# Hashed attention and channel mix on one core: the first head's bucket bits made as rows, and engines and order set anew

## The chip, the cores and the metric

The kernel runs on one core of one Trainium2 chip. The metric is the device time of one execution in microseconds (us), lower is better. The kernel before takes 245.84 us, the median of three runs (245.41 to 245.97). Engines in the text: TensorE (PE; PEld is its weight load), VectorE (DVE), ScalarE (ACT), GpSimd (POOL), SyncE (SP, which only issues DMAs).

## The reference

Two parts run one after the other. First an attention in which a query sees only the keys of its own hash bucket. A bucket is the six signs of the row times a random 64 x 6 matrix. Then a channel mix on the rows of the attention, with the row before.

```python
q, k, v: (4, 8, 768, 64) float32;  proj: (64, 6)
q_bits = (q @ proj) > 0;  k_bits = (k @ proj) > 0          # six bits a row
mask = bucket(q)[:, None] == bucket(k)[None, :]
scores = where(mask, q @ k.T / 8, -1e9)
attn = softmax(scores) @ v                                  # per batch and head
x = attn with the heads side by side                        # (4, 768, 512)
xk, xr = mixes of x and of x shifted by one row, by mu_k and mu_r
r = sigmoid(xr @ w_r)                                       # 512 x 512
out = r * (relu(xk @ w_k) ** 2 @ w_v)                       # 512 x 1024 x 512
```

## The kernel before

**Pairs of heads.** The 32 heads are taken as 16 pairs, n = 0 to 15, four pairs to a batch. q and k of a pair are loaded as rows, 128 partitions by six chunks of 64 columns a head (tiles nat), v likewise (vn). For the scores both have to stand transposed: tile a holds, for each head, 128 partitions by 768 rows of the sequence. Partitions 0 to 63 are the 64 columns scaled by 4 in float16, and partitions 64 to 69 are the six bits as plus or minus a constant. So one product gives the score and, through the bits, a large term that is greatest where the buckets agree. ScalarE's exponential takes the constant off again, and what lies in another bucket comes out as zero.

**Two ways to prepare a pair.** From pair 2 on (`add_prep`) VectorE writes the scaled half (hi, L391) and the rest in float16 (lo, L394) side by side into nh, a DMA transposes nh into a (tr, L398), TensorE multiplies a by the projection (bits, L418), VectorE takes the signs (bx, L421), and GpSimd copies the six rows of each of the four blocks into a (row, L438). hi9, lo9 and so on are those of pair 9. Pairs 0 and 1 (`add_prep_turn`) do without DMA, because the start waits for them. Each block (one side, one head; pair 1 takes both heads in one) goes through: the scaled copy hi into nh (L462); the first turn on TensorE, float32 transposes of nat, three a head (L473, names y); a copy of the result from PSUM, e32 (L477); the bits as rows of the sequence, three small float32 products of 12 columns a head (L481, names x); their signs into nh (ex, L489); the second turn, six float16 transposes of nh (L504, names t); and the copy into a (evt, L509 on VectorE, L511 on ScalarE).

**Scores, softmax, output.** A pair's scores are nine steps of 1024 columns (names sc, L536); each step goes through an exponential on ScalarE (exp, L540). The products with v are six groups of twelve matmuls a pair (oo, L563). v is copied for the first four pairs by GpSimd (va, L343), and summed over the sequence by three additions on GpSimd (vsum, vsumb, vsumc; L349, L352, L355), since its mean is taken off in the later pairs (va on VectorE, L373). rc and ob (L574 to L581) divide by the sum. xt, xs, xz, df, xka, xk, xra, xr (L594 to L636) make the two mixes; xk7 is the last mix that the first products of batch 1 need.

**Channel mix.** Per batch: 16 groups on xk (kp, L651) with a relu on ScalarE (L655) and a square on VectorE (sq, L658); six groups on xr (L671) with a tanh on ScalarE (L674); six groups of eight matmuls on the squares (L684), multiplied on VectorE (os, L691) and stored. The weights arrive as float32 in ten pieces and are cast on GpSimd (wc, L299).

**What sets the order.** Every operation is added to a plan with its engine, and the list ORDER, 1330 numbers written out, is the order in which all are issued; each engine runs its own part of it strictly in that order. BANKS says which bank of PSUM each product uses. Loads, DMA transposes and stores are issued by SP in the same order. ScalarE issues only the first load of k and that of proj. Engines are fixed by the line that adds an operation, by the table TURN (for pairs 0 and 1) and by W_CAST.

In the start, 20 matmuls on zeros (L247, warm-ups) run while the first loads come.

Of the kernel before, what the change touches and what calls it, by code (L numbers as in the profile page):

```python
# [128 lines left out]
def kernel(  # L129
# [13 lines left out]
    nc = tc.nc  # L143
# [188 lines left out]
    def add_v(n):  # L332
# [9 lines left out]
        def f0():  # L342
            nc.gpsimd.tensor_copy(va_t[sa][:, :, :, 0:D], vn)  # L343
# [421 lines left out]
```

## Time and profile before

| | |
|---|---|
| median of three runs | 245.84 us |
| profiled execution, its time | 244.73 us |
| profiled execution, its span | 243.0 us |
| PE busy | 234.2 us, 96% |
| DVE busy | 187.6 us, 77% |
| ACT busy | 182.6 us, 75% |
| POOL busy | 95.9 us, 39% |
| exponentials | 144 of 1.04 us, 139.1 us |
| first exponential starts | 12.78 us |
| granted clock of TensorE | 1.00 throughout |

The span is the part of the profiled execution that the trace covers; its time has some 1.7 us around it. The profiled execution was faster than the median. A matmul's duration in the trace includes its way through the array, so neighbours overlap: four matmuls of 512 columns last 379 ns each but stand 0.86 us apart in the chain. TensorE's share of busy time is therefore no measure of what is left to gain; the stretches with idle time, and who ended it, are.

### The profile page before, as it was taken

Reading aid. Unit: us, or ns where it says so; the run is one execution under the profiler, and the core shown is the slowest. Engines: PE = TensorE matmul, PEld = TensorE weight load, DVE = VectorE, ACT = ScalarE, POOL = GpSimd, SP = SyncE. Lnnn points to the kernel's source line nnn. Section 1 sums busy time; section 2 is a strip of 40 time slices with the busy share of each in tenths; the row PEclk is TensorE's granted clock in tenths of the full one; section 3 lists DMA queues with packets and bytes.
Section 4 is the critical chain, followed back from the end, with each engine's and each line's share of the span. In section 5 each row is a group of like instructions: output and inputs, shape, how many; then the busy total and the mean of one; then the engine's idle time right before and its main releaser. Section 6 shows DMA issues by size and latency. Waiting matters only on the chain.

```text
span 243.0 us, 6250 instructions
## 1 busy us (share of the span) xinstructions
PE 234.2 (96%) x2522; PEld 147.3 (61%) x2522; DVE 187.6 (77%) x388; ACT 182.6 (75%) x242; POOL 95.9 (39%) x150
## 2 busy tenths in 40 slices
PE   8998999999999899999999999999999999999994
PEld 6975676765567446465556665465566765455443
DVE  3489899999899989699999989936745476966142
ACT  3689999999989689698877998777679871165230
POOL 5465797885919673428036230093500000000000
PEclk9999999999999999999999999999999999999999
DMA  6989999999999999999989683464310403041033
GB/s 229 370 243 197 219 259 230 356 204 348 245 217 233 367 281 208 259 272 264 222 195 233 155 162 85 146 114 126 120 46 0 35 3 119 0 173 47 0 131 132
DMA packets 72526, 44.01 MB, mean 181 GB/s; under 512 B 54832, under 2 KB 67504, under 8 KB 72496
## 3 DMA queue, kind: packets, MB, share of 16 engines
q1 hardware_dynamic: 72272, 43.40, 70.7%
q8 instruction: 20, 0.33, 0.6%
q10 hardware_dynamic: 224, 0.20, 0.2%
q14 instruction: 10, 0.08, 0.1%
HBM read 24.12 MB, written 6.29 MB: 125 GB/s over the span
## 4 chain that ended last, share of the span: by engine, by line
PE 55%; DVE 6%; DMA 3%; issue 1%; DVEq 0%
PE ps_all L684 15%; PE ps_all L651 13%; PE ps_all L536 11%; PE ps_all L671 8%; PE ps_all L563 6%; DMA a<-nh 3%; PE ps_all L418 2%; DVE xk L636 1%; DVE tm L633 1%; DVE nh L391 1%; DVE nh L394 1%; DVE df L622 0%; DVE os L691 0%; DVE va L373 0%; DVE bx L421 0%
## 5 line engine op out<-in xcount | busy, mean ns | idle before, releaser
L540 ACT ACTIVATE pt<-ps_all 128x1024 bf16<-128x1024 f32 x144 | 139.1, 1040 | 19.8 <-PE ps_all L536 18.7
L536 PE MATMUL ps_all<-a 128*128 128x256 f16 (+1 forms) x384 | 79.2, 325 | 2.0 <-ACT pt L540 1.1
L438 POOL COPY a<-bx 6x384 f32<-6x384 f32 x56 | 38.9, 696 | 54.5 <-DVE bx L421 42.3
L563 PEld LDWEIGHTS <-pt 128*128 128x128 bf16 x1152 | 43.7, 97 | 11.6 <-issue 2.1
L651 PE MATMUL ps_all<-xk,wk 128*128 128x384 bf16 x256 | 49.6, 326 | 0.3 <-DVE xk L636 0.3
L536 PEld LDWEIGHTS <-a 128*128 128x128 f16 x384 | 33.7, 98 | 24.9 <-issue 3.5
L684 PE MATMUL ps_all<-wv,k 128*128 128x512 bf16 (+2 forms) x208 | 46.7, 363 | 0.0
L563 PE MATMUL ps_all<-va,pt 128*128 128x65 bf16 x1152 | 46.2, 193 | 0.4 <-DVE va L373 0.4
L658 DVE TENSOR_TENSOR k<-kr 128x384 bf16<-128x384 bf16 x64 | 25.8, 424 | 14.1 <-ACT kr L655 13.8
L655 ACT ACTIVATE kr<-ps_all 128x384 bf16<-128x384 f32 x64 | 29.6, 497 | 7.7 <-PE ps_all L651 6.7
L651 PEld LDWEIGHTS <-wk 128*128 128x128 bf16 x256 | 24.0, 98 | 15.5 <-issue 0.3
L674 ACT ACTIVATE rs<-ps_all 128x512 f32<-128x512 f32 x24 | 14.3, 603 | 23.0 <-DVE os L691 11.7
L684 PEld LDWEIGHTS <-k 128*128 128x128 bf16 x208 | 19.6, 98 | 19.1
L691 DVE SCALAR_TENSOR_TENSOR os<-rs,ps_all 128x512 f32<-128x512 f32 (+2 forms) x26 | 16.7, 643 | 14.9 <-PE ps_all L684 10.8
L394 DVE SCALAR_TENSOR_TENSOR nh<-nat,nh 128x1536 f16<-128x1536 f32 (+1 forms) x16 | 25.7, 1607 | 0.2
L671 PE MATMUL ps_all<-wr,xr 128*128 128x512 bf16 x96 | 24.5, 379 | 0.0
L349 POOL TENSOR_TENSOR vt<-vn 128x384 f32<-128x384 f32 x12 | 14.4, 1200 | 10.8 <-DMA vn<-in_v_dram 7.1
L581 DVE TENSOR_TENSOR ob<-ps_all,rc 128x384 bf16<-128x384 f32 x32 | 17.5, 552 | 0.7
L391 DVE TENSOR_SCALAR nh<-nat 128x1536 f16<-128x1536 f32 (+1 forms) x16 | 15.8, 989 | 1.5 <-DMA nat<-in_k_dram 0.9
L671 PEld LDWEIGHTS <-xr 128*128 128x128 bf16 x96 | 8.7, 97 | 9.5 <-issue 0.6
L421 DVE TENSOR_SCALAR bx<-ps_all 128x768 uint16<-128x768 uint16 x14 | 13.3, 952 | 1.2 <-PE ps_all L418 0.8
L373 DVE SCALAR_TENSOR_TENSOR va<-ps_all,vn 128x384 bf16<-128x384 f32 x24 | 12.8, 549 | 1.4 <-ACT pt L540 0.9
(77 smaller groups left out, 190.6 us busy)
## 6 DMA issues: line engine op xcount, KB each, us to landing
vn<-in_v_dram SPq DMA_DIRECT2D x16, 384.0 KB, 5.1
out_dram<-os SPq DMA_DIRECT2D x23, 256.0 KB, 2.5
nat<-in_q_dram SPq DMA_DIRECT2D x15, 384.0 KB, 4.6
nat<-in_k_dram SPq DMA_DIRECT2D x15, 384.0 KB, 5.3
wst<-in_moe_w_k_dram SPq DMA_DIRECT2D x2, 512.0 KB, 7.2
wst<-in_moe_w_r_dram SPq DMA_DIRECT2D x2, 512.0 KB, 6.2
wst<-in_moe_w_v_dram SPq DMA_DIRECT2D x2, 512.0 KB, 5.9
k<-in_moe_w_k_dram SPq DMA_DIRECT2D x1, 512.0 KB, 7.8
```

Of the source, the lines that this page charges most:

```text
L391: nc.vector.tensor_scalar(out=nh[:, :, 0:D], in0=nat.rearrange("p j (c d) -> p (j c) d", d=D), scalar1=QS, scalar2=None, op0=ALU.mult)
L394: nc.vector.scalar_tensor_tensor(out=nh[:, :, D:P], in0=nat.rearrange("p j (c d) -> p (j c) d", d=D), scalar=QS, in1=nh[:, :, 0:D], op0=AL ...
L438: nc.gpsimd.tensor_copy(side_a[side][sa][D : D + NB, j, :].bitcast(FP32), bx_t[sx][32 * i : 32 * i + NB, :].bitcast(FP32))
L536: nc.tensor.matmul(ps[:, lo - s * STEP : hi - s * STEP], side_a["k"][sa][:, j, jc * P : (jc + 1) * P], side_a["q"][sa][:, j, q0 : q0 + hi ...
L540: nc.scalar.activation(out=pt_t[sp][:, s * STEP : (s + 1) * STEP], in_=ps_t[plan.slot[nm]], func=AF.Exp, bias=EBIAS, scale=ESC)
L563: nc.tensor.matmul(oo[:, ic * 65 : ic * 65 + 65], pt_t[sp][:, o : o + P], va_t[sa][:, j, jc, 0 : D + 1], start=(not uc and ic == 0 and jc ...
L581: nc.vector.tensor_tensor(out=ob_t[so][:, :, j * D : (j + 1) * D], in0=oo[:, :, 0:D], in1=rc_t[sr][:, 1, :].unsqueeze(2).to_broadcast([P, ...
L651: nc.tensor.matmul(ps[:, 0:HALF], wk_sb[:, d, fc * P : (fc + 1) * P], xk_t[mx[d]][:, h * HALF : (h + 1) * HALF], start=(d == 0), stop=(d = ...
L655: nc.scalar.activation(out=kr_t[sk], in_=sm(nm)[:, 0:HALF], func=AF.Relu, scale=0.5 ** 0.5)
L658: nc.vector.tensor_tensor(out=k2_t[s2][:, h * HALF : (h + 1) * HALF], in0=kr_t[sk], in1=kr_t[sk], op=ALU.mult)
L671: nc.tensor.matmul(sm(nr), xr_t[mx[d]][:, c * P : (c + 1) * P], wr_sb[:, d, :], start=(d == 0), stop=(d == NDC - 1))
L684: nc.tensor.matmul(sm(nv)[:, x0:x1], k2_t[(b * NFC + fc) % NK2][:, c * P : (c + 1) * P], wv_sb[:, fc, x0:x1], start=(fc == 0), stop=(fc == ...
```

## The change

Four things change together.

1. **First head as rows** (`add_prep_rows`). Head 0 of pair 0 no longer goes through nh and the second turn. After the first turn and its copy (ey0k0, ey0q0) the float32 columns stand with two chunks of 64 columns in the two halves of the partitions. One wide float32 product per side (384 columns; x0k0, x0q0) with a 128 x 64 matrix pz gives the bits already as rows, those of even chunks in one group of partitions and those of odd chunks in another. The signs go from there straight into rows 64 to 69 of a, one instruction per half (ex0q00, ex0q01 on VectorE as sign bits; ex0k00, ex0k01 on ScalarE as Sign), and the scaled columns go straight into rows 0 to 63 (hi0k00 and so on), also one per half.
2. **Zeros**. Two memsets on VectorE become eight smaller ones, two of them on a; pz takes one memset on GpSimd and two small scalings on VectorE.
3. **Engines**. An operation may now name other engines it can run on (`alts`), and the list ENGS says which is taken. From GpSimd to VectorE: wc0, wc8, va0, va1, vsum0b, vsum1, vsum1c, vsum2, vsum3, vsum4, vsum4c, vsum7b, vsum9b, vsum9c, vsum10c, vsum11, vsum11b, vsum11c, vsum13b, vsum13c, vsum14b, vsum15c and the rows row7q1, row7k0, row8k0, row8k1, row9k1, row13q1, row13k0, row15k0. From GpSimd to ScalarE: wc5. From ScalarE to VectorE: ey0q0, ey0q1, ey0k1, evt0k1 and 26 of the 64 relus, three of them in batch 0. From VectorE to ScalarE: hi1k0, one of the two hi2, hi12, hi13, xt15.
4. **Order and banks**. ORDER (now 1339 numbers) and BANKS are new lists. On SP's queue the loads come as q0, q of pair 1, q1, k1, k of pair 1, k of pair 2, v of pair 0; before they came as q0, q of pair 1, k1, q1, k of pair 1, v of pair 0, k of pair 2. The second turns of head 1 (k and q) now stand ahead of the first scores on TensorE; before, that of q stood behind the first step. Three of the warm-ups stand behind the first transposes. On VectorE va0 stands ahead of ex0q01 and of the bits of head 1 for k; on ScalarE the scale of pair 2's k stands ahead of the first exponential.

```diff
 ORDER = [
...
+ENGS = [
+    "DVE", "POOL", "POOL", "POOL", "POOL", "ACT", "POOL", "POOL", "DVE", "POOL", "ACT", "ACT", "ACT", "DVE", "ACT", "ACT", "DVE", "DVE",
...
+        if alts:
+            e = ENGS[self.flex] if ENGS else eng
+            self.flex += 1
+            fn = lambda f=fn, e=e: f(e)
...
-    TURN = {(n, side, j): ("ACT", "DVE", "DVE", "ACT" if side == "k" and n == 0 else "DVE") for n in range(2) for side in "qk" for j in range(2)}
-    PARTS = {0: ((0, 1), (1, 2)), 1: ((0, 2),)}
-    W_CAST = ["POOL"] * 10
+    PARTS = {0: ((1, 2),), 1: ((0, 2),)}
+    ROWS = ((0, 0),)
+    SIGN = {(0, 0): "k"}
...
+    pz = buf([P, 64], FP32, "pz")
...
+    def copy_on(e, o, i_):
+        nc.scalar.copy(o, i_) if e == "ACT" else tt_on(e).tensor_copy(o, i_)
...
-    for i in range(NNH):
-        add("DVE", 0.8, lambda i=i: nc.vector.memset(nh_t[i][:, :, D + NB : P].bitcast(FP32), 0.0), w=[("nz", i)], name=f"nz{i}")
+    for n, j in ((0, 0), (0, 1), (1, 0), (1, 1)):
+        for side in "qk":
+            if (n, j) in ROWS:
+                add("DVE", 0.4, lambda n=n, j=j, side=side: nc.vector.memset(side_a[side][n][D:P, j, :].bitcast(FP32), 0.0),
+                    w=[("ab", side, n, j, h) for h in range(2)], name=f"nz{n}{side}{j}")
...
+        add("POOL", 1.4, f_c, r=keys, w=[("w" + which, c) for c in range(c0, c0 + n_)], port=1, name=f"wc{i}",
+            alts=(("ACT", ACT_C(1024), 0), ("DVE", DVE_C(1024, 2), 1)))
...
+            add("POOL", 0.91, f0, r=[("vn", s)], w=[("va", sa, 0), ("va", sa, 1)], port=1, name=f"va{n}", alts=(("DVE", DVE_C(768, 2), 1), ("ACT", ACT_C(768), 0)))
...
+    def add_prep_rows(n, j):
+        s, sh, sa = n % NQ, n % NNH, n % NAQ
+        sign = SIGN.get((n, j))
+        for i, side in enumerate("kq"):
+            nat, a = side_nat[side][s], side_a[side][sa]
+            a32 = side_nh[side][sh].rearrange("p c d -> p (c d)").bitcast(FP32)[:, j * HALF : (j + 1) * HALF]
...
+            def tp(ny=ny, nat=nat):
+                for g in range(3):
+                    nc.tensor.transpose(sm(ny)[:, g * P : (g + 1) * P], nat[:, j, g * P : (g + 1) * P], idf)
+            def e32(e, ny=ny, a32=a32):
+                copy_on(e, a32, sm(ny)[:, 0:HALF])
+            def bb(nx=nx, a32=a32, i=i):
+                nc.tensor.matmul(sm(nx)[64 * i : 64 * i + 64, 0:HALF], pz, a32, start=True, stop=True)
...
+            for e in range(2):
+                cols = a[:, j, :].rearrange("p (g e q) -> p g e q", e=2, q=P)[:, :, e, :]
+                def hi(g, a32=a32, cols=cols, e=e):
+                    scale_on(g, cols[0:D], a32[e * D : (e + 1) * D, :].rearrange("p (g q) -> p g q", q=P))
+                def ex(nx=nx, cols=cols, e=e, i=i, side=side, mag=mag):
+                    p0 = 64 * i + 32 * e
+                    o, i_ = cols[D : D + NB], sm(nx)[p0 : p0 + NB, 0:HALF].rearrange("p (g q) -> p g q", q=P)
+                    if side == sign:
+                        nc.scalar.activation(out=o, in_=i_, func=AF.Sign, bias=1e-30)
+                        return
+                    nc.vector.tensor_scalar(out=o.bitcast(U16),
...
+                    else:
+                        nc.vector.tensor_scalar(out=kr_t[sk], in0=i_, scalar1=0.0, scalar2=0.5 ** 0.5, op0=ALU.max, op1=ALU.mult)
...
             add_proj()
+            add_prep_rows(0, 0)
             add_prep_turn(0)
```

More of the change, by code (lines that the diff above doesn't have):

```diff
@@ L230, with tt_on, scale_on @@
     plan = Plan()
+    def tt_on(e):
+        return nc.gpsimd if e == "POOL" else nc.vector
+    def copy_on(e, o, i_):
+        nc.scalar.copy(o, i_) if e == "ACT" else tt_on(e).tensor_copy(o, i_)
+    def scale_on(e, o, i_):
+        if e == "ACT":
+            nc.scalar.activation(out=o, in_=i_, func=AF.Copy, scale=QS)
+        else:
+            tt_on(e).tensor_scalar(out=o, in0=i_, scalar1=QS, scalar2=None, op0=ALU.mult)
     add = plan.add
@@ L292, in f_w, with f_c @@
             nc.sync.dma_start(out=stage, in_=src)
-        def f_c(stage=stage, dst=dst, i=i):
-            e = W_CAST[i]
-            if e == "ACT":
-                nc.scalar.copy(dst, stage)
-            else:
-                (nc.gpsimd if e == "POOL" else nc.vector).tensor_copy(dst, stage)
+        def f_c(e, stage=stage, dst=dst):
+            copy_on(e, dst, stage)
         add("SP", 0.5, f_w, w=keys, at=0.75, svc=1.45, name=f"wl{i}")
-        add(W_CAST[i], {"POOL": 1.4, "ACT": ACT_C(1024), "DVE": DVE_C(1024)}[W_CAST[i]], f_c, r=keys,
-            w=[("w" + which, c) for c in range(c0, c0 + n_)], port=int(W_CAST[i] != "ACT"), name=f"wc{i}")
+        add("POOL", 1.4, f_c, r=keys, w=[("w" + which, c) for c in range(c0, c0 + n_)], port=1, name=f"wc{i}",
+            alts=(("ACT", ACT_C(1024), 0), ("DVE", DVE_C(1024, 2), 1)))
     SRC = {"q": q, "k": k}
@@ L424, in g @@
                 scalar1=0x8000, scalar2=0x5400, op0=ALU.bitwise_and, op1=ALU.bitwise_or)
-        add("PE", 2 * MM(S) + 0.13, f, r=["p1", "p2"] + [("a", side, sa, j) for side, j in blocks],
+        add("PE", 2 * MM(S) + 0.13, f, r=["p1", "p2"] + [("a", side, sa, j, h) for side, j in blocks for h in range(2)],
             w=[(nm,)], take=("sc", nm, 0), name=nm)
@@ L435, in add_bits, with row @@
                 continue
-            def row(i=i, side=side, j=j):
-                nc.gpsimd.tensor_copy(side_a[side][sa][D : D + NB, j, :].bitcast(FP32), bx_t[sx][32 * i : 32 * i + NB, :].bitcast(FP32))
-            add("POOL", 0.55, row, r=[("bx", sx)], w=w, port=1, name=f"row{n}{side}{j}")
+            def row(e, i=i, side=side, j=j):
+                copy_on(e, side_a[side][sa][D : D + NB, j, :].bitcast(FP32), bx_t[sx][32 * i : 32 * i + NB, :].bitcast(FP32))
+            add("POOL", 0.55, row, r=[("bx", sx)], w=w, port=1, name=f"row{n}{side}{j}", alts=(("DVE", DVE_C(384), 1),))
     def add_prep_turn(n):
@@ L456, in add_prep_turn, with hi @@
                 whole = m == 2
-                def hi(nat=nat, nh=nh, e_hi=e_hi, j0=j0, j1=j1):
-                    o = nh[:, j0 * NSC : j1 * NSC, 0:D]
-                    i_ = nat[:, j0:j1, :].rearrange("p j (c d) -> p (j c) d", d=D)
-                    if e_hi == "DVE":
-                        nc.vector.tensor_scalar(out=o, in0=i_, scalar1=QS, scalar2=None, op0=ALU.mult)
-                    else:
-                        nc.scalar.activation(out=o, in_=i_, func=AF.Copy, scale=QS)
+                def hi(e, nat=nat, nh=nh, j0=j0, j1=j1):
+                    scale_on(e, nh[:, j0 * NSC : j1 * NSC, 0:D], nat[:, j0:j1, :].rearrange("p j (c d) -> p (j c) d", d=D))
                 def place(ny=ny, whole=whole):
@@ L513, in add_prep_turn, with ev @@
-                    add(e_ev, DVE_C(S, 2) if e_ev == "DVE" else ACT_C(S), ev, r=[(nm,)],
-                        w=[("a", side, sa, j)] + [("ab", side, sa, j, h) for h in range(2)], give=[nm], name="ev" + nm)
+                    def ev(e, nm=nm, a=a, j=j):
+                        copy_on(e, a[:, j, :], sm(nm)[:, 0:HALF].bitcast(FP16))
+                    add("PE", 0.48, tr, r=["idh", ("nhh", side, sh, j), ("nhl", side, sh, j), ("nz", sh, side, j)], w=[(nm,)], take=("sm", nm, 0), name=nm)
+                    add("DVE", DVE_C(S, 2), ev, r=[(nm,)],
+                        w=[("a", side, sa, j, h) for h in range(2)] + [("ab", side, sa, j, h) for h in range(2)], give=[nm], name="ev" + nm, alts=(("ACT", ACT_C(S), 0),))
@@ L528, in add_scores @@
             need = [("ab", "q", sa, j, h) for j in heads for h in range(2)]
-            need += sorted({("ab", "k", sa, ch // NSC, (ch % NSC) // 3) for ch in chunks})
+            half = (lambda c: c % 2) if n in FIRSTS else (lambda c: c // 3)
+            for ch in chunks:
+                need += [x for x in (("ab", "k", sa, ch // NSC, half(ch % NSC)), ("a", "k", sa, ch // NSC, half(ch % NSC))) if x not in need]
             def f(nm=nm, s=s):
@@ L543, in add_scores @@
             add("PE", sum(MM(b - a) for a, b in pieces(s)), f,
-                r=need + [("a", side, sa, j) for side in "qk" for j in heads],
+                r=need + [("a", "q", sa, j, h) for j in heads for h in range(2)],
                 w=[(nm,)], take=("sc", nm, 0), name=nm)
@@ L609, in add_pv @@
             add("PE", 6 * 0.056, ft, r=["idb", ("ob", so, 0), ("ob", so, 1)], w=[(nm,)], take=("sm", nm, 0), name=nm)
-            add("DVE", DVE_C(768, 2), fx, r=[(nm,)], w=[("xt", sx)], give=[nm], name=f"xt{n}")
+            add("DVE", DVE_C(768, 2), fx, r=[(nm,)], w=[("xt", sx)], give=[nm], name=f"xt{n}", alts=(("ACT", ACT_C(768), 0),))
         else:
@@ L662, in add_moe @@
                         w=[(nm,)], take=("sm", nm, 1) if ds[0] == 0 else None, name=nm)
[L663 removed]
+                add("ACT", ACT_C(HALF), g, r=[(nm,)], w=[("kr", sk)], give=[nm], name=f"relu{b}_{fc}", alts=(("DVE", DVE_C(HALF), 0),))
                 add("DVE", DVE_C(HALF, 2), g2, r=[("kr", sk)], w=[("k2", s2, h)], port=1, name=f"sq{b}_{fc}")
@@ L701, in add_proj @@
         for e in range(2):
+            add("DVE", 0.1, lambda e=e: nc.vector.tensor_scalar(out=pz[e * D : (e + 1) * D, e * 32 : e * 32 + NB], in0=pj, scalar1=-1.0, scalar2=None, op0=ALU.mult),
+                r=["pj"], w=["pz"], port=1, name=f"pz{e}")
+        for e in range(2):
             add("POOL", 0.2, lambda e=e: nc.gpsimd.tensor_scalar(out=pw[e * D : (e + 1) * D, e * NB : (e + 1) * NB], in0=pj, scalar1=-1.0, scalar2=None, op0=ALU.mult),
```

102 lines of the change are left out of this document (60 added, 42 removed), and 120 rows, old and new, of tables (BANKS, ORDER).

## The prediction

> **What bounds the kernel now.** I read the stretches first (busy time of each engine in 12 us pieces; columns PE, PEld, DVE, ACT, POOL, clock, DMA share, GB/s), because a share of the whole span mixes three stages.
>
> ```profile
> 6.00:12.00 6.00, 6.00 (x65) 5.87 (x64) 3.08 (x10) 3.96 (x6) 3.01 (x6) 1.00 1.05 371
> 12.00:24.00 12.00, 10.97 (x114) 7.71 (x114) 10.48 (x16) 11.03 (x12) 7.54 (x9) 1.00 0.92 226
> ...
> 36.00:48.00 12.00, 11.60 (x187) 7.89 (x185) 11.86 (x20) 12.00 (x15) 9.67 (x12) 1.00 1.10 301
> ...
> 96.00:108.00 12.00, 11.19 (x112) 5.77 (x108) 9.91 (x22) 9.26 (x11) 2.76 (x6) 1.00 1.08 267
> 108.00:120.00 12.00, 11.66 (x139) 7.29 (x141) 11.79 (x25) 10.28 (x14) 7.13 (x11) 1.00 1.05 241
> 120.00:132.00 12.00, 12.00 (x137) 7.25 (x130) 11.37 (x27) 8.90 (x14) 4.76 (x8) 1.00 0.98 222
> ```
>
> From 120 us TensorE has no idle time until 239.7. What happens there on other engines costs nothing as long as it stays so; the end is 120 us plus the TensorE work still to do. So a gain must come from before 120: the start (first exponential at 12.78), the stage in which ScalarE is full (36 to 60), and the waits of TensorE from 24 to 120, 3.3 us by these rows. VectorE is the third candidate: full at 36 to 48, and from 108 to 120 hardly less.
>
> The start, as the weight loads of TensorE (time, length, engine, line, count):
>
> ```profile
> 4.38 1.77 PEld L473 LDWEIGHTS ps_all<-pt,nat 128*128 128x128 f32 x15
> 6.28 1.41 PEld L481 LDWEIGHTS ps_all<-pw,pt 128*128 128x128 f32 x12
> 7.53 0.40 PEld L473 LDWEIGHTS ps_all<-pt,nat 128*128 128x128 f32 x3
> 7.89 0.75 PEld L481 LDWEIGHTS ps_all<-pw,pt 128*128 128x128 f32 x6
> 8.48 0.43 PEld L504 LDWEIGHTS <-nh 128*128 128x128 f16 x6
> 8.87 0.64 PEld L473 LDWEIGHTS ps_all<-pt,nat 128*128 128x128 f32 x6
> 9.47 0.75 PEld L481 LDWEIGHTS ps_all<-pw,pt 128*128 128x128 f32 x6
> 10.06 0.77 PEld L504 LDWEIGHTS <-nh 128*128 128x128 f16 x12
> 10.78 1.42 PEld L481 LDWEIGHTS ps_all<-pw,pt 128*128 128x128 f32 x12
> 12.04 0.42 PEld L536 LDWEIGHTS <-a 128*128 128x128 f16 x3
> ```
>
> Each row starts where the one before ends: from 4.38 to 12.04, when the first scores go out, TensorE never stands still. Differences of the starts give the prices: a group of three f32 transposes 0.36 (six: 0.60), the bits of one head's side 0.60 (1.25 for two), one second turn 0.37.
>
> Last, who waits for VectorE: a piece of the chain that ended last (start, length, what), and who waited for whom (us, times, longest).
>
> ```profile
> 90.21 7.27 DMA a<-nh
> ```
> ```profile
> PE ps_all L418 <- DMA a<-nh: 1.3, 2, 0.8
> ...
> PE ps_all L651 <- DVE xk L636: 0.3, 1, 0.3
> ```
>
> TensorE waits 0.8 us at 97.5 for the transposed block of pair 9, sent at 90.21 right after VectorE's lo9 (90.13), and 0.3 us, until 118.09, for xk7 (the chain goes from L636 to L651 there). Both waits are VectorE's lateness.
>
> **The change, part by part.**
>
> *First head on TensorE.* Gone: two small products (1.25) and two second turns (0.74). New: two wide f32 products of 384 columns. No row has one. Bounds: 384 bf16 columns issue in 0.163 (four matmuls of L651 take 0.65 on the chain) and a small f32 product shows as two matmuls, so at least 0.33; three f32 transposes are 384 f32 columns in 0.36 to 0.38, two such passes are 0.76. I take 0.70, near the f32 rows. The Trainium skill, page "FP8 and Floating Point Precision", section "TensorE Precision Notes", says a true FP32 product makes four passes; four times 0.163 would be 0.65, and the first scores 0.1 earlier than below. No run here shows it yet.
>
> Three of the warm-up matmuls move behind the first transposes, which then start when the first k load lands (4.03, where VectorE's first L462 starts). The new order sums to: 4.03 + 0.37 + three warm-ups of 0.18 (18 take 3.20) + 0.37 + 0.60 + 0.37 = 6.28; two wide products 7.68; 0.36 + 0.60 + 0.60 + 0.60 = 9.84; the bits of pair 1's q 1.26 = 11.10; both second turns of head 1, 0.74, now ahead of the first scores: 11.84, against 12.04. With 0.33 a product it is 11.10, with 0.76 11.96.
>
> *What stands in front on VectorE.* The copy of v for pair 0 (va0) moves from GpSimd to VectorE, ahead of the last bit row of head 0 and of the bits for k of head 1. Its load is now the seventh on SP's queue instead of the sixth; the seventh was issued at 4.02, after a wait, the sixth at 3.12. The load landed at 8.98 (GpSimd's L343 started then), so now near 9.9. Copy 0.55 (L462, same shape), bit row 0.55 (just over half of L421's 0.95), bits 0.20: 11.2. The second turn of k can thus start at 11.2, not 11.10; the scores go out at 11.95. ScalarE has the scale of pair 2's k (0.8, by L477 at this size) ahead of the first exponential; it waits for that second turn, about 11.65, and ends at 12.45. First exponential: 11.95 + 0.74 (12.78 - 12.04) = 12.69, a gain of 0.1. Should the load land no later than before, the gain is 0.2; if 384 KB more ahead of it cost a further 1.0 (this size moves at 0.39 MB/us in the start), it is a loss of 0.9. The load's landing decides, not TensorE. The 0.18 that ScalarE waits before its fourth exponential goes, since head 1 is ready: 0.2.
>
> Six transposed copies on VectorE become four, but eight small memsets, four PSUM copies, two bit rows, va0 and va1 and three sums come on. Up to the bits of pair 2 (23.42) that is about 4 us more on VectorE, whose idle time to 24 us is 8.4. I cost it at nothing; its cover is those gaps, and L421 there waits for TensorE anyway.
>
> *VectorE from 29.9 (after the bits of pair 3) to xk7 (118.05).* Busy 82.6 of 88.2. Added before xk7: two casts of weights (0.65 each, from L391's 0.55 for 768 columns), two sums of 384 (0.5), four of 128 (0.2), five rows (0.2 to 0.45), three relus (0.5): 5.6 to 6.9. Gone or put later: hi12 (0.95), xr5 (0.6), rc8 and ob8 (0.8), two va9 (1.0), mc9 and the two mu (0.3): 3.7. Net +1.9 to +3.2; I take +2.5.
>
> Against this, GpSimd loses 30 of its operations, 29% of its work here. Its work makes VectorE slow; the same instruction with GpSimd busy (48 to 84) and silent (180 to 206):
>
> ```profile
> L604 DVE COPY xt<-xt 128x127 bf16<-128x127 bf16 x3 | 1.9, 637 | 0.0
> ```
> ```profile
> L604 DVE COPY xt<-xt 128x127 bf16<-128x127 bf16 x2 | 0.4, 188 | 0.0
> ```
>
> L622 goes from 1100 to 558 ns, L658 from 534 to 346. Over the instructions of this stretch that is some 10 us. If it falls with GpSimd's work, 3 us come back; at worst nothing. So the demand is 82.6 + 2.5 - 3 = 82.1, between 81.5 and 85.8.
>
> The order on TensorE now has the first matmul on xk7 earlier: three groups of scores (0.43 to 0.54), L671's four matmuls (0.86), four of L684 (0.86) and three groups of L563 (0.36) come behind it instead of ahead, 4.2 us by the chain. So xk7 is needed at 118.09 - 0.3 - 4.2, less some 0.2 gained before: 113.4. There are 83.5 us from 29.9. Without idle time VectorE is 1.4 us early, with the half of its 5.6 us of idle left, 1.4 late. Behind a late xk7 TensorE's whole queue stands, scores too, and through them ScalarE. I take no wait, because work put in front fills waits of an in-order engine; both ends go into the range. For lo9 the same sum: added 4.3, gone 1.8, relief 2: +0.5 with 2.95 idle to fill, while TensorE asks 0.55 earlier. The 0.8 wait becomes between 0 and 1.5; I take 0.4, a gain of 0.4.
>
> *ScalarE* from 60 to 110 loses three relus (1.3) and gets a cast and hi12 (0.9 and 1.3): +0.9 where it is 77 to 92% busy. No cost; the cover is this idle time, and if gone, 0.9. *After 120* some 20 relus and some sums come onto VectorE, at 6 to 9 us busy of 12 from 156; no TensorE wait, no cost. The tail behind the last matmul (3.3 us) is unchanged.
>
> **Sum.** -0.1 (first exponential) -0.2 (fourth) -0.4 (pair 9) = -0.7. Against the profiled span that is 242.3 for 243.0, its time 244.0 for 244.73. The median of the runs shown is 1.11 above the profiled run; from it, 245.84 - 0.7 = 245.1.
>
> **Rivals.**
>
> *VectorE late for xk7 (slower).* For it: 94% busy already, the net addition, and the earlier need. Against: GpSimd's relief. The point is 83.5 us of demand plus idle; with half of the idle time and the relief 1.4 late, with half of it and no relief 4.4. Taking the middle, 2.6, less the 0.3 that is waited now: +2.3, less 0.3 of the start's gain: 247.8.
>
> *The gain is given back.* v's load lands 0.5 later than taken and eats the start, or pair 9's wait stays. 245.8.
>
> *VectorE freed.* GpSimd's work was what slowed it: with the 3 us of relief and little idle time xk7 and lo9 are early, and the 3.3 us of waits between 24 and 120 mostly go. With 2.3 of them: 245.84 - 2.3 - 0.3 = 243.2. The Trainium skill's "GPSIMD Engine Reference", section "Specifications", says the two engines share SBUF interfaces; by that rule the slower rows above shrink with every operation taken off GpSimd, and the trace agrees (637 against 188 ns).
>
> **How the numbers follow.** Forecast (0 to 1.5 faster) 0.38; VectorE late 0.36; given back 0.14; freed 0.12. About 0.2% (0.49 us) is what a measurement of this kernel tells from no change. Faster by more: 0.30 of the forecast, 0.12 of the freed, 0.02 of the third = 0.44. Within: 0.08 + 0.05 + 0.07 = 0.20. Slower: 0.31 + 0.05 = 0.36. Range: 243.4 (most of the freed case) to 248.0 (late by 2.6, start's loss not added); the forecast alone 244.3 to 245.8.
>
> **What would show it.** The wide products near 0.7 us each; first scores near 11.95 and first exponential near 12.7; va0 on VectorE waiting for v's load until about 9.9; xk7 before 113.5 with no wait of L651's successor for it; VectorE's L604 and L622 shorter at 48 to 84. A wait of TensorE over 1 us before 120, or VectorE over 97% from 30 to 113, makes it wrong on the slow side; no wait at all from 24 to 120 on the fast side.

## The result

The changed kernel takes 250.13 us, the median of four executions (248.84 to 251.03); the kernel before took 245.91 beside it (245.41 to 246.96). The ratio is 1.0152, with a 95% interval from 1.0111 to 1.0193: slower by 3 to 5 us. The prediction was 245.1, with a range up to 248.0. A ratio compares undisturbed executions only, so it need not be the quotient of the medians beside it.

The stretches of the profiled execution after (251.03 us, the longest of the four; span 249.2), in the columns of those shown of before:

```profile
12.00:24.00 12.00, 11.40 (x117) 7.37 (x115) 11.20 (x22) 12.00 (x15) 2.39 (x4) 1.00 1.14 248
36.00:48.00 12.00, 10.94 (x170) 7.21 (x168) 11.94 (x19) 11.85 (x14) 7.88 (x9) 1.00 1.06 307
60.00:72.00 12.00, 10.88 (x126) 6.64 (x123) 11.83 (x21) 9.87 (x15) 7.47 (x11) 1.00 0.98 256
72.00:84.00 12.00, 9.46 (x129) 6.40 (x126) 11.87 (x22) 8.56 (x12) 8.07 (x8) 1.00 0.93 218
84.00:96.00 12.00, 11.62 (x97) 6.43 (x97) 10.82 (x27) 8.84 (x12) 4.27 (x4) 0.86 0.88 205
108.00:120.00 12.00, 12.00 (x131) 7.11 (x129) 11.86 (x24) 10.52 (x13) 4.04 (x6) 1.00 0.90 199
```

Before, the rows from 72 and from 84 read:

```profile
72.00:84.00 12.00, 11.24 (x172) 7.74 (x170) 11.38 (x32) 10.11 (x15) 9.60 (x13) 1.00 1.13 281
84.00:96.00 12.00, 12.00 (x123) 7.23 (x122) 11.03 (x14) 10.24 (x13) 7.58 (x9) 1.00 1.07 247
```

From 72 to 84 TensorE (first column) falls from 11.24 to 9.46 with VectorE full (third), and from 84 to 96 the granted clock is 0.86. The groups in which TensorE makes the bits of a pair are good milestones, since these seven stand at nearly the same place of its order in both kernels (of those left out behind bits9, bits10 and bits11 come later in the order, bits13 and bits14 earlier). Their starts, from the timelines:

| | bits2 | bits6 | bits7 | bits8 | bits9 | bits12 | bits15 |
|---|---|---|---|---|---|---|---|
| before | 22.5 | 55.1 | 70.2 | 82.8 | 97.5 | 127.5 | 169.1 |
| after | 22.4 | 55.7 | 71.0 | 88.7 | 103.1 | 132.6 | 174.9 |
| later by | -0.1 | 0.6 | 0.8 | 5.9 | 5.6 | 5.1 | 5.8 |

So nothing is lost in the start, 0.8 us up to bits7, and 5.1 us in the one stage from bits7 to bits8; about 0.65 us of that is work which now stands ahead of bits8 (28 weight loads for products on xk instead of 24, four products taking 0.65). The rest of the kernel keeps the delay. This is what happens in that stage. VectorE's timeline (start, length, line, tiles, count):

```profile
77.38 3.46 DVE L692 SCALAR_TENSOR_TENSOR xr<-df,mur,xt 128x768 bf16<-128x768 bf16 x2
80.76 1.18 DVE L727 TENSOR_TENSOR k<-kr 128x384 bf16<-128x384 bf16 x1
81.97 1.08 DVE L259 COPY a<-bx 6x384 f32<-6x384 f32 x1
83.08 0.36 DVE L727 TENSOR_TENSOR k<-kr 128x384 bf16<-128x384 bf16 x1
```

GpSimd's:

```profile
77.30 1.05 POOL L259 CAST wv<-wst 128x1024 bf16<-128x1024 f32 x1
78.32 1.70 POOL L386 TENSOR_TENSOR vt<-vn 128x384 f32<-128x384 f32 x1
79.97 1.76 POOL L259 CAST wv<-k 128x1024 bf16<-128x1024 f32 x1
81.68 1.17 POOL L259 CAST wv<-os 128x1024 bf16<-128x1024 f32 x1
```

ScalarE's and TensorE's:

```profile
82.03 0.49 ACT L722 ACTIVATE kr<-ps_all 128x384 bf16<-128x384 f32 x1 [2.35 <-DVE k L727]
82.42 1.02 ACT L605 ACTIVATE pt<-ps_all 128x1024 bf16<-128x1024 f32 x1
```
```profile
83.50 0.23 PE L404 MATMUL ps_all<-vs,ones 128*128 128x128 bf16 x1 [2.24 <-ACT pt L605]
...
84.38 0.58 PE L601 MATMUL ps_all<-a 128*128 128x256 f16 x2 [0.42 <-DVE ob L646]
84.77 2.44 PE L716 MATMUL ps_all<-xk,wk 128*128 128x384 bf16 x7
```

Two xr on VectorE take 1.73 us each, a square 1.18 and a copied row 1.08, all while GpSimd works through four operations. Before, the stage had one xr, 1.19 us beside a sum and a copied row on GpSimd:

```profile
76.93 1.19 DVE L627 SCALAR_TENSOR_TENSOR xr<-df,mur,xt 128x768 bf16<-128x768 bf16 x1
```

A relu on ScalarE waits 2.35 us for the buffer that a late square frees, the exponential behind it in ScalarE's order waits with it, and TensorE stands 2.24 us for the bank that this exponential frees. Behind that its seven matmuls on xk take 2.44 us (1.30 for the same seven in a profile without the wait). The stretches of 3.4 us around it:

```profile
80.83:84.24 3.41, 0.90 (x13) 0.36 (x10) 3.31 (x8) 1.41 (x2) 2.01 (x2) 1.00 0.23 80
84.24:87.68 3.44, 3.30 (x22) 1.95 (x22) 3.31 (x11) 1.84 (x3) 0.00 (x0) 0.50 0.44 71
```

The clock is halved for 3.44 us, which takes at most 1.72 us of TensorE's work. From bits7 to bits8 TensorE is idle for 2.96 us (0.76 before). The 5.16 us are thus 2.20 of more idle time, up to 1.72 of clock, 0.65 of reordered work and some 0.6 that these rows don't place.

The halved clock is not needed for the loss. One of the four executions after has a mean clock of 1.00 and took 248.84 us, still 2.9 above the median before; the three at 0.991 to 0.993 averaged 250.4.

### The profile page after: what moved, and what is told of

Same layout as the page of the kernel before. It is cut to its first block, busy times and chain, and to the rows that moved or that the text cites. A ratio compares the mean times of both kernels' runs of the same rounds, so it can differ in the third digit from the quotient of the medians.

```text
span 249.2 us, 6249 instructions
## 1 busy us (share of the span) xinstructions
PE 237.2 (95%) x2502; PEld 147.1 (59%) x2502; DVE 207.4 (83%) x448; ACT 179.3 (72%) x223; POOL 74.9 (30%) x120
## 4 chain that ended last, share of the span: by engine, by line
PE 64%; DVE 20%; DMA 8%; POOL 3%; issue 3%; SPq 0%; DVEq 0%; POOLq 0%
PE ps_all L753 15%; PE ps_all L716 14%; PE ps_all L601 13%; PE ps_all L628 8%; PE ps_all L740 6%; DMA a<-nh 5%; DVE nh L431 3%; DMA nat<-in_q_dram 3%; PE ps_all L455 3%; DVE k L727 2%; POOL a L259 2%; DVE bx L458 2%; DVE xr L692 2%; PE ps_all L282 2%; PE ps_all L511 1%
## 5 line engine op out<-in xcount | busy, mean ns | idle before, releaser
L601 PE MATMUL ps_all<-a 128*128 128x512 f16 (+1 forms) x384 | 81.8, 326 | 3.1 <-DVE bx L458 0.9
L259 POOL COPY a<-bx 6x384 f32<-6x384 f32 x48 | 37.5, 782 | 68.6 <-DVE bx L458 36.8
L716 PE MATMUL ps_all<-xk,wk 128*128 128x384 bf16 x256 | 50.3, 331 | 1.2 <-DVE kr L724 0.9
L753 PE MATMUL ps_all<-wv,k 128*128 128x512 bf16 (+2 forms) x208 | 46.2, 363 | 0.0
L716 PEld LDWEIGHTS <-wk 128*128 128x128 bf16 x256 | 24.5, 99 | 19.3 <-issue 3.7
L722 ACT ACTIVATE kr<-ps_all 128x384 bf16<-128x384 f32 x38 | 18.5, 499 | 22.7 <-DVE k L727 11.3
L458 DVE TENSOR_SCALAR bx<-ps_all 128x768 uint16<-128x768 uint16 x14 | 13.3, 952 | 3.5 <-PE ps_all L455 3.5
L724 DVE TENSOR_SCALAR kr<-ps_all 128x384 bf16<-128x384 f32 x26 | 14.1, 550 | 2.2 <-PE ps_all L716 1.7
L740 PEld LDWEIGHTS <-xr 128*128 128x128 bf16 x96 | 9.3, 98 | 10.0
L386 POOL TENSOR_TENSOR vt<-vn 128x384 f32<-128x384 f32 x10 | 11.4, 1137 | 11.4 <-DMA vn<-in_v_dram 9.5
```

The source lines that it names most:

```text
L259: nc.scalar.copy(o, i_) if e == "ACT" else tt_on(e).tensor_copy(o, i_)
L458: nc.vector.tensor_scalar(out=bx_t[sx][0:rows].bitcast(U16), in0=ps_t[plan.slot[nm]][0:rows, 0:S].bitcast(U16).rearrange("p (c e) -> p c e ...
L601: nc.tensor.matmul(ps[:, lo - s * STEP : hi - s * STEP], side_a["k"][sa][:, j, jc * P : (jc + 1) * P], side_a["q"][sa][:, j, q0 : q0 + hi ...
L716: nc.tensor.matmul(ps[:, 0:HALF], wk_sb[:, d, fc * P : (fc + 1) * P], xk_t[mx[d]][:, h * HALF : (h + 1) * HALF], start=(d == 0), stop=(d = ...
L722: nc.scalar.activation(out=kr_t[sk], in_=i_, func=AF.Relu, scale=0.5 ** 0.5)
L740: nc.tensor.matmul(sm(nr), xr_t[mx[d]][:, c * P : (c + 1) * P], wr_sb[:, d, :], start=(d == 0), stop=(d == NDC - 1))
```

## The experiments

In each, "place" means this stage at 77 to 88 us. Behind the start, the change sets 56 operations on other engines and has another order. The first four runs set three theories against each other: one place at 77 to 88 us, with its halved clock (1); VectorE's load as a whole (2); the new start (3). Theories A to D came after them and are told in the expectations.

**The start alone.** The first 168 places of the changed order, with its engines and banks there; behind them order, engines and banks of before.

```diff
-ORDER = changed list
+ORDER = changed list[:168] + (list of before without these)
-ENGS, BANKS = changed lists
+ENGS, BANKS = as changed for these 168, else as before
```

> Only the start of the change (rows for head 0, its engines, the first 168 places of the new order); order, engines and banks behind that as in the kernel before. Theory 1 (the 4 us are lost at one place, 77 to 88 us, where VectorE comes late with squares and TensorE stands and loses its clock): no loss here, 245.6 to 246.6. Theory 2 (VectorE's load as a whole is too much): the same, since its load is back. Theory 3 (the start itself costs: first exponential 13.01 instead of 12.78, and the wait for the bits of pair 3): 247 to 249.

Measured: 245.83 us (244.53 to 249.21), ratio 0.9961 (0.9929 to 0.9993). The start costs nothing and brings about 1 us; the loss lies wholly behind it.

**Two xr later, relus back, GpSimd's operations back.** Three edits of the changed kernel. First:

```diff
-        return [self.ops[i] for i in ORDER]
+        order = [i for i in ORDER if i not in (282, 332)]      # xr2, xr3
+        k = order.index(559) + 1                               # behind row7q1
+        order[k:k] = [282, 332]
+        return [self.ops[i] for i in order]
```

> The changed kernel with two VectorE operations (xr2, xr3: 3.46 us together at 77.4) moved behind row7q1, so that the squares in front of which they stand come earlier; nothing else. Theory 1: the squares free the relu's tiles 3 us earlier, TensorE's wait of 2.4 us at 81 and the fall of the granted clock behind it go: 245.8 to 247.5. Theory 2: the work is still there and is only waited for elsewhere: 249 to 250.5.

Second:

```diff
             self.flex += 1
+            if name.startswith("relu"):
+                e = "ACT"
```

> The changed kernel with all 64 relus on ScalarE, as before; order and all else as changed. Three of them lie ahead of 84 us, 1.5 us of VectorE. Theory 1: the squares at 77 to 82 come 1 to 1.5 us earlier, the wait shrinks to about 1 us and the clock may hold: 247 to 249. Theory 2: 26 relus, 13 us of VectorE, are gone: 246 to 247.5. If ScalarE is what binds: 250 or more.

Third:

```diff
             self.flex += 1
+            if eng == "POOL" and name not in ("va0", "va1", "vsum0b", "vsum1", "vsum1c"):
+                e = "POOL"
```

> The changed kernel with the 25 operations behind the start that had gone from GpSimd to VectorE (and wc5, to ScalarE) on GpSimd again. VectorE loses some 8 us of work, of which 4 lie ahead of 84 us; GpSimd gets them. Theory 1: the squares come earlier, but GpSimd's work beside them slows them; between 246.5 and 250. Theory 2: 246 to 248. If the moved operations were worth it on VectorE (GpSimd's contention is what slows it): 251 or more.

Measured: 248.99 (ratio 1.0089, 1.0039 to 1.0138), 253.60 (1.0295, 1.0258 to 1.0332) and 253.02 us (1.0258, 1.0223 to 1.0294). Taking work off VectorE made it worse twice, so its load as a whole is not what costs the time; but each edit also put that work on another engine, and the waits show that this is what it cost. With the relus back, TensorE waits in seven places for exponentials (6.1 us in all), where the changed kernel has 2.5. With GpSimd's operations back, a sum on GpSimd comes late behind four weight casts, and TensorE waits for it:

```profile
PE ps_all L406 <- POOL vs L394: 3.5, 1, 3.5
```
```profile
49.76:53.12 3.36, 0.03 (x1) 0.00 (x0) 0.00 (x0) 2.20 (x3) 3.23 (x5) 1.00 1.20 203
53.12:56.52 3.40, 3.19 (x42) 2.67 (x42) 1.60 (x5) 0.00 (x0) 0.66 (x2) 0.50 0.97 294
```

Here too the clock is halved for 3.40 us behind the wait. Moving the two xr gave 1.1 us of the 4 by the medians (the intervals of the two ratios overlap): they took 1.95 us for both once GpSimd was done, but the output block behind them was later, and TensorE waited 1.99 us for it at bits8.

**Engines alone, order alone.**

```diff
 ORDER, BANKS = as in the start-only kernel
+ENGS = changed list throughout
```

> The order after the start is that of before, with before's PSUM banks; all engines are those of the change (56 operations behind the start run on another engine than in the start-only kernel, most of them from GpSimd and ScalarE to VectorE). Two theories of the loss behind the start. A: the new order makes it, because it puts xr2, xr3, squares and a copied row one behind the other on VectorE at 77 to 85 us while GpSimd casts weights, with relus on ScalarE that wait for their buffers ahead of exponentials. Then the old order with the new engines has no such place and stays within 1 us of the start-only kernel: 245 to 247 us. B: the 20 us of work that VectorE gets make it late in any order: 249 us or more, with TensorE waits for VectorE between 30 and 120 us of 3 us or more beyond the start-only kernel's.

```diff
 ORDER, BANKS = changed lists
+ENGS = as in the start-only kernel
```

> The order is that of the change throughout; behind the start the 56 operations go back to the engines of before (relus to ScalarE, sums, rows and casts to GpSimd). Theory A (the order makes the loss, the engines moved soften it): slower than the changed kernel, since undoing the relus alone gave 253.6 and GpSimd's operations alone 253.0; I expect 253 to 258. Theory B (VectorE's load makes it): faster than the changed kernel, 246 to 249.

Measured: 265.60 (ratio 1.0791, 1.0756 to 1.0827) and 256.70 us (1.0472, 1.0415 to 1.0528). With the start alone at 245.8 and the changed kernel at 250.1, these are the four corners. The engines cost 20 us on the old order and bring 6.6 on the new one. My question, order or engines, was badly put. They fit only each other: theory A's 245 to 247 for the first corner was wrong by 19, and theory B's 246 to 249 for the second by 8; for the other corner each was right.

**Idle matmuls in the wait.**

```diff
+            if nm == "mean7":
+                for _ in range(10):
+                    nc.tensor.matmul(ps_t[3][:, 0:512], ones, wk_sb[:, 0, 0:512], start=True, stop=True)
             nc.tensor.matmul(ps[:, 0:P], ones, vf, start=True, stop=True)
```

> The changed kernel with ten idle matmuls of 512 columns (0.216 us each by the 1.03 us for four or five on the timeline, about 2.1 us) put on TensorE just ahead of the product that waits 2.24 us at 81 us; their result is never read. Theory A says that half of this place's loss is the granted clock, which falls to 0.56 for 4 us behind the wait: with TensorE busy in the wait the clock stays at 1.00 at 84 to 88, and the time falls by 1 to 2 us against the changed kernel (about 248.3 to 249). The rival, that the clock costs nothing here because VectorE and ScalarE are the ones late at 84 to 88: within 0.4 us of the changed kernel, or slower by what the fillers overrun.

Measured: 250.76 us (249.24 to 252.02), ratio 1.0191 (1.0158 to 1.0225). It brought nothing, so what the halved clock costs by itself is not settled by this run. But the profiled execution, the fastest of the six and the only one with a mean clock of 1.00 (the others have 0.993), points to the cause. In it the first of GpSimd's four operations was late, because its weights landed late:

```profile
78.13 1.04 POOL L259 CAST wv<-wst 128x1024 bf16<-128x1024 f32 x1 [2.23 <-DMA wst<-in_moe_w_v_dram]
```
```profile
76.04 1.94 DVE L695 SCALAR_TENSOR_TENSOR xr<-df,mur,xt 128x768 bf16<-128x768 bf16 x2
77.90 0.35 DVE L730 TENSOR_TENSOR k<-kr 128x384 bf16<-128x384 bf16 x1
78.28 1.10 DVE L259 COPY a<-bx 6x384 f32<-6x384 f32 x1
```

The same two xr take 1.94 us with GpSimd still, 3.46 beside it; the row behind them, beside the cast, again takes 1.10. The stage from bits7 to bits8 takes 15.4 us there (17.7 after), with the idle matmuls' 2.1 us in them. They can't simply be taken off. The second score product behind them needs an output block (after, TensorE waits 0.42 us for it), and VectorE ends that at 81.35, so only some 0.8 us would come off there. That two xr are short with GpSimd still gave theory C, that the four operations beside VectorE make the loss, and the next experiment.

**GpSimd held back.** One small copy makes GpSimd wait for a square on VectorE before its four operations; nothing is taken away.

```diff
-        def f_c(e, stage=stage, dst=dst):
+        def f_c(e, stage=stage, dst=dst, i=i):
+            if i == 9:
+                nc.gpsimd.tensor_copy(tb[:, 1:2], k2_t[5][:, HALF : HALF + 1])
             copy_on(e, dst, stage)
```

> The changed kernel with one thing added: GpSimd first copies one column of the last square of the sixth feature block before it casts the weights wc9, so its four operations wc9, vsum8, wc6 and wc7 (77 to 83 us in the changed kernel's trace) start only when xr2, xr3, the squares and the two row copies on VectorE are done; GpSimd has 8 us without work behind them. Theory C: those four operations beside VectorE make the loss at 77 to 88 us (two xr took 3.46 us there, and 1.94 in the run with idle matmuls, where the weights landed 2.2 us later and GpSimd stood still beside them). C expects xr2 and xr3 at 1.0 us each, squares near 0.35, TensorE's wait of 2.24 us gone and its clock at 1.00 from 80 to 92; time 246.5 to 248.5, against 250.1 of the changed kernel. The rival, that VectorE is late there by its amount of work alone and the later casts slow what comes behind: 249.5 or more.

Measured: 246.18 us (245.87 to 248.60, twelve executions), ratio 1.0016 (0.9983 to 1.0048), against 1.0152 without the hold. VectorE, then GpSimd, in its profile:

```profile
79.16 1.94 DVE L694 SCALAR_TENSOR_TENSOR xr<-df,mur,xt 128x768 bf16<-128x768 bf16 x2
81.02 0.34 DVE L729 TENSOR_TENSOR k<-kr 128x384 bf16<-128x384 bf16 x1
81.40 0.35 DVE L259 COPY a<-bx 6x384 f32<-6x384 f32 x1
81.78 0.36 DVE L729 TENSOR_TENSOR k<-kr 128x384 bf16<-128x384 bf16 x1
```
```profile
83.80 0.30 POOL L338 CAST tb<-k 128x1 f32<-128x1 bf16 x1 [4.77 <-DVE k L729]
84.03 1.03 POOL L259 CAST wv<-wst 128x1024 bf16<-128x1024 f32 x1
85.04 1.30 POOL L388 TENSOR_TENSOR vt<-vn 128x384 f32<-128x384 f32 x1
86.28 1.03 POOL L259 CAST wv<-k 128x1024 bf16<-128x1024 f32 x1
87.27 1.04 POOL L259 CAST wv<-os 128x1024 bf16<-128x1024 f32 x1
```

The five instructions that took from 77.38 to 83.44 take from 79.16 to 82.14: 2.98 us instead of 6.06. TensorE has no wait there, its clock stays at 1.00, and bits7 to bits8 take 13.2 us, which is the 12.6 of before and the 0.65 of reordered work. (This profiled execution, 248.60 us, is the longest of the twelve, with a mean clock of 0.986: it fell in the start, which is told below, and so all of it stands later. The kernel with the hold and idle matmuls in the start, whose profile has a clock of 1.00 throughout, takes 13.3 us in this stage.) GpSimd does the same operations 4 to 5 us later, measured from the first xr, and TensorE shows no wait for them. This is theory C's result in each point: four operations that were in no hurry, put beside VectorE's tightest stretch, made almost all of the loss. The hold moves the four together; which of them does most was not tried apart.

**ScalarE's order.** The relu moved behind the exponential it held up.

```diff
+        order = [i for i in ORDER if i != 379]                 # relu0_5
+        order.insert(order.index(569) + 1, 379)                # behind exp6_3
```

> The changed kernel with one relu of the sixth feature block moved on ScalarE from ahead of the exponential that TensorE waits for to behind it. If ScalarE's order makes the wait at 81 us (the relu waits 2.35 us for its buffer and holds the exponential), the wait of 2.24 us shrinks to less than 0.5 and the time falls by 2 to 4 us, to 246 to 248. If VectorE makes it, TensorE next waits for the row copy that VectorE ends at 83.05, 0.4 us before the exponential ended: the time stays within 0.7 us of the changed kernel.

Measured: 249.44 us (248.88 to 251.89), ratio 1.0141 (1.0092 to 1.0190). TensorE passes the old wait and stops at the next results of VectorE:

```profile
82.22 0.39 PE L603 MATMUL ps_all<-a 128*128 128x512 f16 x1 [1.80 <-DVE a L261]
83.50 0.38 PE L603 MATMUL ps_all<-a 128*128 128x256 f16 x2 [0.89 <-DVE ob L648]
```

So the chain through the relu was only the way by which VectorE's lateness arrived; two more lead to the same place. Six buffers instead of four between relus and squares would have tested the same link; they need 209.3 KB a partition where there are 207.9, so there is no run of it.

This run says something on the clock, too. VectorE's instructions at the place take what they took after (3.46, 1.19 and 1.08 us), but in its profile the clock stays at 1.00, and bits7 to bits8 take 16.2 us against 17.7. By these two profiles the halved clock is worth about 1.6 us of the stage, an estimate, and the waits the rest.

**The start's clock.** Five of the ten profiles with the new start told so far show the clock halved in the start, between 10 and 18 us. (The expectation below counts four of seven; there were eight by then.) Idle matmuls between the small products there, in the kernel with GpSimd held back and in the start-only kernel:

```diff
+                    if nx in ("x0q1", "x0k1", "x1q0"):
+                        for _ in range(2):
+                            nc.tensor.matmul(sm("warm")[:, 0:256], wz[:, 0:P], wz[:, 0:256], start=True, stop=True)
```

> As the run with GpSimd held back, and six idle matmuls of 256 columns (0.11 us each) between the small products of 12 columns in the start (two each behind the bits of the second side of head 1 and of pair 1). Theory D: in about half the executions of every kernel with the new start the granted clock halves once between 8 and 15 us, because TensorE has only those small products there (four of the seven profiles with the new start show it, for 3.4 us each and once 6.8); it costs some 1 to 2 us. D expects mean clocks of 0.997 or more in nearly all runs and 0.5 to 1.5 us less than without the fillers: 246 to 247.5. The rival, that the clock falls elsewhere or costs nothing in the start: the same mean clocks of 0.991 to 0.993 and no gain, or a loss of the 0.6 us of the fillers.

> The start-only kernel (245.83, ratio 0.9961) with the same six idle matmuls in its start. In its ten runs six had a mean clock of 0.997 or more and took 245.2 on average, four had 0.985 to 0.993 and took 247.0. D expects clocks of 0.997 or more in nearly all runs and a ratio of 0.992 to 0.995, the best kernel so far. The rival: clocks as before and a ratio of 0.996 to 0.999, since the fillers cost up to 0.6 us ahead of the first scores.

Measured: 246.63 (ratio 1.0020, 0.9987 to 1.0052) and 245.97 us (0.9993, 0.9967 to 1.0019). Half of theory D holds. All 24 executions with the fillers have a mean clock of 0.997 or more, where without the fillers six of twelve and four of ten had 0.993 or less. The price was wrong: no time is gained. With GpSimd held back the six executions at 1.00 averaged 246.1 us, the four at 0.991 to 0.993 246.4, and two at 0.986 248.5. Only the profiled one of them can be looked into, where the clock falls in the start alone; if the others fall there too, one fall costs 0.3 us, and the fillers as much or more.

**The same hold in the start-only kernel.** There TensorE waits 1.53 us for an output block at 82.3, behind a df of 1.39 us and a square of 1.19 that stand beside GpSimd's casts.

```diff
+            if i == 8:
+                nc.gpsimd.tensor_copy(tb[:, 1:2], k2_t[5][:, HALF : HALF + 1])
```

> The start-only kernel (245.83, ratio 0.9961) with the same kind of hold: GpSimd copies one column of the last square of the sixth feature block before its four casts of the value weights (79.97 to 84.4 us in the start-only trace), so they begin when VectorE is done with df4 and the squares ahead of the output block that TensorE waits 1.53 us for at 82.3. Theory C says that GpSimd's casts make that wait: df4 takes 1.39 us there and the square behind it 1.19, against 0.55 and 0.35 beside an idle GpSimd. C expects both near those, the wait of 1.53 near 0.2, and a ratio of 0.990 to 0.994. The rival: the casts come too late for the first value products (88.7 us in the start-only trace) and the ratio is 0.996 or more.

Measured: 246.04 us (243.77 to 247.95; before beside it 246.02), ratio 0.9961 (0.9933 to 0.9989). The mechanism is there:

```profile
79.62 0.54 DVE L689 TENSOR_TENSOR df<-xt 128x768 bf16<-128x768 bf16 x1
80.09 0.35 DVE L729 TENSOR_TENSOR k<-kr 128x384 bf16<-128x384 bf16 x1
...
80.65 0.98 DVE L648 TENSOR_TENSOR ob<-ps_all,rc 128x384 bf16<-128x384 f32 x2
```

The wait is gone, and bits8 starts at 82.4 instead of 84.5. The time is not: 0.990 to 0.994 was expected, and 0.996 is what the start-only kernel has without the hold. In the profiled execution, one of the four longest, the 2.1 us are lost again at bits9. The transposed block of pair 9, sent at 89.78, takes 8.82 us to land there, TensorE waits 2.3 us for it, and its clock halves. Start alone and start with hold are faster than both kernels, than the one before by 0.4% each; that the hold adds to it is not shown.

## Why the prediction was wrong

*What bounds the kernel.* "The end is 120 us plus the TensorE work still to do" held: TensorE idles 0.5 us from 120 to 180, the delay at bits9 (5.6) is the delay at bits15 (5.8) and nearly that of the span (6.2). The loss did come from before 120, in VectorE's lateness.

*Wide products.* 0.70 each was too much. Four matmuls from 7.24 to 8.03, when the next transposes start, are 0.40 for each product of 384 columns, inside the bounds of 0.33 and 0.76. By the four passes of the Trainium skill's "FP8 and Floating Point Precision", section "TensorE Precision Notes", it would be 0.65; the trace disagrees, and 0.40 counts.

*The first exponential.* Predicted 12.69, it came at 13.01 against 12.78. The first load of k landed at 4.36 rather than 4.03; va0 waited 0.39 us for v's load and started at 10.18 (9.9 predicted); the scores went out at 12.24 (11.95 predicted). The gap before the fourth exponential went, as said: four run in 3.77 us from 13.01. Bits2 are 0.1 us early, and the start alone is worth 0.4%. So the first exponential moved the other way than predicted, by 0.2 us, the gap came out about right, and both are small. The 1.0 us that the start alone brings is more than the prediction's 0.3 and was not taken apart.

*VectorE from 29.9 to xk7.* This is the step that failed. The demand was put at 82.6 + 2.5 - 3 = 82.1 us, with bounds to 85.8. It measures 85.3 of the 89.0 us from 29.80 to 118.80. Of these, 3.08 are what the five instructions at 77.38 took over their time with GpSimd still. Without this place the sum would have been 82.2, and in the kernel with the hold and the idle matmuls in the start it measures 81.2 of 83.6 us, where 82.1 of 83.5 were predicted. So additions and relief came out together (how much of it each is, no run says), and the term of 3 us "if it falls with GpSimd's work" was wrong where it mattered. I priced contention by the amount of GpSimd's work, but it depends on what stands beside what. GpSimd's busy time in this stretch fell from 57.5 to 45.4 us, 21% and not the 29% that I took, and some VectorE instructions did get shorter from 48 to 84 us (df 1100 to 544 ns, the copies of xt 637 to 186), but the mean xr went from 1071 to 1527 ns and the squares from 534 to 698. The rule cited from the Trainium skill's "GPSIMD Engine Reference", section "Specifications", says which instructions suffer, those with two SBUF inputs or in a mode that uses both ports. The trace agrees: the square with two SBUF inputs takes 0.35 or 1.18 us, while the output block, read from PSUM, takes 0.51 to 0.56 in the profiles before, after and with the hold. Not every such instruction gets longer: lo at 59.94 before, with two SBUF inputs, takes 1.75 us, its median, and the sum on GpSimd that starts 0.65 us behind it takes 1.96 (1.18 for the next one). I had read the rule as a share that shrinks evenly.

*"I take no wait, because work put in front fills waits of an in-order engine."* For xk7 that came out: it was ready at 118.80, TensorE took it at 119.07 without a wait, being 5.6 us late itself. It came out with TensorE on time as well: in the kernel with the hold and the idle matmuls in the start xk7 is ready at 113.37, and TensorE takes it at 113.63 (113.4 predicted):

```profile
112.13 1.24 DVE L706 TENSOR_TENSOR xk<-tm,xt 128x768 bf16<-128x768 f16 x1
113.63 0.81 PE L721 MATMUL ps_all<-xk,wk 128*128 128x384 bf16 x4
```

But a demand summed over 88 us says nothing on a place inside it, and the wait arose there.

*Pair 9's 0.8 us.* It went entirely (0.4 predicted), with the hold too, where no wait for a DMA remains at bits9.

*ScalarE and after 120.* Costing ScalarE at nothing was right: its new idle time is waiting for VectorE's squares (11.3 us in all), and giving it the relus back cost 3.5 us more. After 120 the cost is not quite nothing: 0.5 us in two waits, and in the profile with the hold and the idle matmuls in the start, which gets there earlier, TensorE idles 1.6 us from 120 to 180.

*The rivals.* "VectorE late" had the right engine and side, but at xk7 and for 2.6 us. (The middle of its 1.4 and 4.4 is 2.9, so it should have read 248.1, just above the end of the range.) It missed the two things that made it 4 to 5: TensorE stops at a result in the middle of the stage, and its clock halves behind the wait. No step of the prediction had the clock in it. Of its own signs for the slow side one came, a wait of TensorE over 1 us before 120; VectorE from 30 to 113 was busy for 95.7%, not over 97. "VectorE freed" had the right lever: holding GpSimd back won 4 us, though by when it runs and not by how much.

What stays open: why the changed kernel with the hold is still 1.3 us behind the start-only kernel by the ratios, whose intervals overlap. TensorE's idle time from 120 to 180 (1.6 us as said above, against 0.3 in the start-only kernel) is about that much, but no run took these waits out.

## What to carry to other kernels

Where VectorE is full, price GpSimd's work by which of VectorE's instructions it runs beside. Lay the two timelines over each other, stage by stage, and let work that is in no hurry start behind the tight stretch; one small dependency did that here for 4 us. Don't test engines and order found together one by one, since either alone can be far worse than both. Behind a wait of TensorE of 2 us the clock may halve for 3.4 us, up to 1.7 us more: price the wait with that in the range. It doesn't always come.

## What the hardware showed

The granted clock fell in blocks of one length: 3.44 us behind the place, 3.40 behind the wait for the sum, and in the start of the kernel with GpSimd held back for twice that:

```profile
7.80:11.24 3.44, 3.07 (x28) 3.02 (x28) 1.32 (x5) 2.21 (x5) 0.00 (x0) 1.00 1.05 385
11.24:18.00 6.76, 6.72 (x35) 4.99 (x34) 6.05 (x12) 4.61 (x7) 2.27 (x4) 0.50 1.00 292
```

The Trainium skill, "TensorE: Matmul & The Clock Gate", Part 1, describes a window of 3.4 us that runs freely, with half the clock after an idle window until a busy one. The length agrees. That the window has to be idle does not: TensorE was busy for 0.90 of 3.41 us ahead of the fall at the place, and for 3.07 of 3.44 by the first of these rows, which holds transposes and many of the products of only 12 columns. Six idle matmuls of 256 columns among those products, 0.6 us of work, went with a mean clock of 0.997 or more in all 24 executions, so what counts there is apparently not the busy time that the profile shows. A wait doesn't always bring the fall, either: in the run with the relu moved, TensorE was busy for 0.40 us of the 3.08 from 80.42 to 83.50, and the clock stayed at 1.00. The free run would explain why the same kernel falls in some executions and not in others; no run here shows it.
